# Sliding-window attention inside a four-layer kernel: vector operations over four rows at once, and the query copy moved

## Chip, cores and metric

The kernel runs on one core of one Trainium2 chip. The metric is the device time of one execution in microseconds (us); a kernel's time is the median of its runs.

## What is computed

Four residual layers stand one after the other, attention, Fourier mixing, attention, Fourier mixing, on x of 2048 rows by 640 columns in float32, each behind a layer normalisation. The attention is local and dilated: 32 heads of 20 columns, and each row sees 8 rows, itself and those 2, 4, ... 14 rows before it.

```python
qkv = (x @ wqkv) split in q, k, v, 32 heads of 20
idx = pos[:, None] - arange(8)[None, :] * 2          # masked where idx < 0
logits = einsum("bhsd,bhswd->bhsw", q, kg) * 20 ** -0.5
attn = softmax(logits, axis=-1)
o = einsum("bhsw,bhswd->bhsd", attn, vg)
x = x + o @ wo                                       # layer A
a = x @ dft_hid_re.T;  b = x @ dft_hid_im.T
x = x + (dft_seq_re @ a - dft_seq_im @ b)            # layer B, on the normalised x
```

## The kernel before

The rows are permuted on the host, even rows first, so that a step of 2 becomes a step of 1. They are cut into 4 chunks of 512 rows; partition p of a chunk holds 4 neighbouring rows, j = 0 to 3. All matmuls are done in three passes over a high and a low float32r part of each operand (`PASSES`); ACT makes the high part (`t_hi`, `c_hi`, `ln_hi`) and DVE or POOL the low one by a subtraction (`c_lo` L901, `wo_lo` L555, `ln_lo` L866).

**A layer of attention (`layer_a`).** PE makes q, k and v of a chunk's row j and a quarter of the heads per group (`qkv_mm` L354), ACT moves them out of PSUM (`qkv_evac` L361), and DMAs store them to DRAM. From there they come back as windows: one contiguous piece per partition of 11 rows holds all that 4 query rows need (`w_load` L409), in a ring of 5 slots named `win`. The window arithmetic does not use PE. It is cut into 32 units u, 8 for each chunk; a unit is 4 heads (80 columns, `FE`) for 4 rows per partition. In the last chunk, units 24 to 31 (`PAIRED`), a unit is 8 heads for 2 rows, with two windows of 9 rows a side; the chunk's first row pair is then finished before its second.

Each unit goes through these steps, most of them twice, once for each half of two rows (`jp`):
- `q_load` and `q_copy` (L396, ACT): the query comes from DRAM into tile `qs` and is copied into the PSUM bank `pq`. The same bank holds the mask, the maximum, the sum and the probabilities `pp`, in other columns.
- `qk_mul`: DVE multiplies query and key window into a product of 2 x 8 x 80 = 1280 elements per partition (L423), POOL adds the first 10 columns of each head to the last 10 (L425).
- `qk_red`: DVE sums those 10 into the logits (L431).
- `soft` parts 0 to 2 on DVE (mask, maximum, subtraction), `soft_exp` on ACT (L439), parts 3 to 5 on DVE (sum, reciprocal, probabilities L456). These are done once per unit.
- `av_mul`: DVE multiplies probabilities and value window (L461).
- `av_tree`: POOL sums the 8 window rows pairwise in three steps, L476, L477 and L478, the last into the output tile `oo` (`zo`). The last half of the last unit is summed on DVE.

The products lie in four tiles `pr0` to `pr3` of 1280 elements taken in turn (`prod`), keys' and values' products mixed.

The output is transposed on PE, split, multiplied by wo (`wo_mm` L501), added to x by DVE (`wo_add` L151) and stored. While a layer of attention runs, PE also starts the next Fourier layer's first product (`z_mm` L916), whose matrix is split by `c_hi` and `c_lo` in the first layer of attention and read back split in the second.

**The order.** Everything in a layer of attention is issued in an order written out by hand, on all engines. `at(step, phase, fn, ...)` enters a call into a plan; the steps run from -7 to 66, and within a step the phases run in the order of `PHASES`. Each engine's queue is in that order, so an instruction that waits holds up what stands behind it on its engine. Unit u has steps 2u and 2u + 1 for its two halves of `qk_mul`; the logit sums follow a step later (`red1`, `red0`), the first half of the softmax and the exponent are at 2u + 2, the second half at 2u + 3, and the two halves of `av_mul` and `av_tree` at 2u + 3 (`av1`) and 2u + 4 (`av0`). `q_copy` of unit u is at step 2u - 1 in phase `qc`, behind `av1` and behind ACT's own phases. The last transposes of a layer are at step `TA` = 65 and after the loop (67).

The Fourier layers use the same tiles again: `load_w` puts four of the five parts of the imaginary matrix into `pr0` to `pr3`, and the first chunk's input rows are loaded into `pr0` to `pr3` at the start of the kernel.

Of the kernel before, what the change touches and what calls it, by code (L numbers as in the profile page):

```python
# [20 lines left out]
D = 640  # L21
H = 32
DH = 20
# [25 lines left out]
)  # L49
TA = 65  # L50
NWARM = 18
# [20 lines left out]
def tile_layers(ctx: ExitStack, tc: tile.TileContext, x, wqkv, wo, cs, wre, wim, out):  # L72
# [161 lines left out]
    def layer_a(li, stats, handoff, prev):  # L234
# [6 lines left out]
        xnT = {}  # L241
        pcnt = [0]
        mt = {}
# [14 lines left out]

        def prod():
            pcnt[0] += 1  # L260
            return T([P, 2, W, FE], f"pr{pcnt[0] % 4}")

# [136 lines left out]
        def w_load(u, t, i=None):  # L399
            c = u // NE  # L400
            e, jp = half(u, i or 0)
            r0 = (c % 2) * 512
            if i is not None:
                r0 += 2 * jp
            n = SLOTS if i is None else SLOTS - 2
            b = kvb[e // 2][c // 2][e % 2, t, r0 : r0 + n, :]
            src = bass.AP(tensor=b.tensor, offset=b.offset, ap=[[NJ * FE, P], [1, n * FE]])
            w = wtile([P, SLOTS * FE])
            nc.sync.dma_start(w[:, : n * FE], src)  # L409
            if i is None:  # L410
                for x in range(2):
                    win[(u, x, t)] = (w, 2 * x * FE)
            else:
                win[(u, i, t)] = (w, 0)
# [5 lines left out]
        def qk_mul(u, jp):  # L420
            pr = prod()
            q = qs[u][:, 2 * jp : 2 * jp + 2].unsqueeze(2).to_broadcast([P, 2, W, FE])
            nc.vector.tensor_tensor(pr, q, wview(u, jp, 0, [[1, FE]]), op=ALU.mult)  # L423
            pv = pr.rearrange("p j w (h d) -> p (j w h) d", d=DH)
            nc.gpsimd.tensor_tensor(pv[:, :, 0:10], pv[:, :, 0:10], pv[:, :, 10:20], op=ALU.add)  # L425
            prq[(u, jp)] = pv

        def qk_red(u, jp):
            if jp == 0:
                lgs[u] = T([P, NJ, W, HE], "lg", bufs=2)  # L430
            nc.vector.tensor_reduce(  # L431
                lgs[u][:, 2 * jp : 2 * jp + 2].rearrange("p j w h -> p (j w h)"),
                prq.pop((u, jp))[:, :, 0:10],
                axis=AX.X,
                op=ALU.add,
            )
# [21 lines left out]

        def av_mul(u, jp):
            pr = prod()  # L460
            nc.vector.tensor_tensor(  # L461
                pr.rearrange("p j w (h d) -> p j w h d", d=DH),
                lgs[u][:, 2 * jp : 2 * jp + 2].unsqueeze(4).to_broadcast([P, 2, W, HE, DH]),
                wview(u, jp, 1, [[DH, HE], [1, DH]]),
                op=ALU.mult,
            )
            avq[(u, jp)] = pr

        def av_tree(u, i):
            c = u // NE  # L470
            e, jp = half(u, i)
            if e == 0:
                oo[(c, jp)] = T([P, 2, D], f"zo{(2 * c + jp) % 4}")
            pr = avq.pop((u, i))
            g = nc.vector if (u, i) == (NG - 1, 1) else nc.gpsimd
            g.tensor_tensor(pr[:, :, 0:4], pr[:, :, 0:4], pr[:, :, 4:8], op=ALU.add)  # L476
            g.tensor_tensor(pr[:, :, 0:2], pr[:, :, 0:2], pr[:, :, 2:4], op=ALU.add)  # L477
            g.tensor_tensor(oo[(c, jp)][:, :, e * FE : (e + 1) * FE], pr[:, :, 0], pr[:, :, 1], op=ALU.add)  # L478

# [123 lines left out]
        def prologue_first():  # L603
            wq_begin(0)
            for j, (k0, k1) in enumerate(((0, 3), (3, 5))):
                x_load(0, j, f"pr{j}")
                for k in range(k0, k1):
                    wq[(0, k)] = wq_load1(0, k)
            for j in range(2, NJ):
                x_load(0, j, f"pr{j}")  # L610
            for q in (1, 2, 3):
# [144 lines left out]
        for c, w, xtags in (  # L756
# [3 lines left out]
            for j in range(NJ):  # L760
                if c == 2:
                    tp(48, "o", c, j, 0, 3, ("xt", "t0", "t1", "m0")[j], 0, ("ot", "s1", "r1_2", "r1_2")[j])
                    tp(52, "o", c, j, 3, 5, f"aux{j // 2}", 256 * (j % 2))
                else:
                    tp(58 if j < 2 else TA, "o", c, j, 0, 3, f"aux{j % 2}", 0, ("ot", "s1", "zo0", "zo1")[j])
                    tp(60 if j < 2 else 67, "o", c, j, 3, 5, "aux0" if j < 2 else "pq", 256 * (j % 2))
                if j < len(w):
# [8 lines left out]
        for ph in ("peT0", "hi", "peL", "actL"):  # L776
            plan.pop((67, ph))
        at(66, "pe3w", wo_mm, c, 2, ("aux0", "aux1"), 0, 2, 0, 3)
        for i in range(2):
            at(65, "dmas", *((handoff.cw_load, 0) if first else (handoff.c_get,)), 14 + i)  # L780
        at(65, "dmar", r_load, c, 2, "xr")
        at(66, "dmar", r_load, c, 3, "xa")
# [4 lines left out]
        last = 66  # L787
        thirds = [t for t, n in ZTHIRDS[ly].items() for _ in range(n)]
# [14 lines left out]
        else:  # L803
            at(63, "dmac", handoff.c_get, 13)

        PHASES = (
            "peT0 dma evac hi pe peL pe2 fin red0 dma2 qk sA sB av0 sD red1 sE sC exp evacA actL evacO actl sF av1 qc"
            " dmaw dmas misc dmac dmar pe3w pe3"
        ).split()
        with tc.manual_schedule(engines=ENGINES):  # L810
# [7 lines left out]
            pc_pe(67)  # L818
            pc_hi(67)
            pc_lo(67, True)  # L820
            wo_mm(c, 2, None, 0, 2, 3)
# [22 lines left out]
    class LayerB:  # L844
# [79 lines left out]
        def load_w(self):  # L924
            self.wr = T([P, 2, KD, D], "r2a", F32R)
            self.wi = []
            for k in range(KD):
# [3 lines left out]
                if k < 4:  # L931
                    wt = T([P, 2, D], f"pr{k}", F32R)
                    hl = (wt[:, 0], wt[:, 1])
# [383 lines left out]
```

## Time and profile before

| | us |
|---|---|
| median of 3 runs (lowest to highest) | 1812.42 (1808.80 to 1813.48) |
| the profiled execution's own time | 1810.4 |
| its span, first to last instruction | 1808.5 |
| PE busy, DVE busy, ACT busy, POOL busy | 1746.1, 1380.1, 818.9, 640.6 |
| L423 and L461, DVE, 128 times each | 189.8 and 190.8 busy, mean 1483 and 1491 ns |
| L431, DVE, 128 times | 103.9 busy, mean 811 ns |
| L425, L476, L477, POOL | 183.4, 200.9, 114.4 busy, mean 1433, 1595, 908 ns |

PE is TensorE, DVE VectorE, ACT ScalarE, POOL GpSimd, SP SyncE, which issues most DMAs. A busy time is summed over the whole span, which holds two layers of attention and two Fourier layers; POOL works almost only in the attention. A line of the profile names the source line of the kernel before (L423), what an instruction writes and reads, and, in square brackets or behind an arrow, how long its engine was idle ahead of it and what ended that. Granted clock is the share of full speed that the throttle allows PE.

### The profile page before, as it was taken

The numbers are of one execution on the slowest core, as the hardware profiler recorded it, in microseconds if no ns is written. First come the engines' busy times: TensorE is split into PE (matmuls) and PEld (weight loads), VectorE is DVE, ScalarE is ACT, GpSimd is POOL, SyncE is SP. The second block draws the span as 40 slices with busy tenths as digits, with TensorE's granted clock in tenths as the row PEclk, the third lists the DMA queues.
The fourth block names the chain that finished last, engine by engine and source line by source line (L and its number), as shares of the span: only waits on it lengthen the run. The fifth ranks groups of instructions, "written<-read, shape, count | busy, mean of one in ns | idle before, by whom it ended". The sixth has DMA issues, their size and how long they took to land.

```text
span 1808.5 us, 26471 instructions
## 1 busy us (share of the span) xinstructions
PE 1746.1 (97%) x8798; PEld 1508.9 (83%) x8798; DVE 1380.1 (76%) x2129; ACT 818.9 (45%) x1708; POOL 640.6 (35%) x597
## 2 busy tenths in 40 slices
PE   9999997989999999999999999999899999999999
PEld 6879886777887887888888889877788888888888
DVE  5899899888768767767739988887777677676673
ACT  5544544544445445445533334444434443443441
POOL 3799898960000000000008987899400000000000
PEclk9999998999999999999999999999999999999999
DMA  6776667647789689677647856687687766876761
GB/s 233 224 263 208 208 203 247 218 164 280 273 267 332 223 270 336 221 258 229 215 132 226 278 181 199 200 296 261 218 295 257 259 226 225 265 231 223 259 210 52
DMA packets 273738, 423.59 MB, mean 234 GB/s; under 512 B 22688, under 2 KB 152736, under 8 KB 273344
## 3 DMA queue, kind: packets, MB, share of 16 engines
q1 hardware_dynamic: 270400, 419.92, 70.0%
q10 hardware_dynamic: 3200, 1.97, 0.4%
q8 instruction: 70, 1.15, 0.2%
q14 instruction: 68, 0.56, 0.1%
HBM read 336.66 MB, written 85.14 MB: 233 GB/s over the span
## 4 chain that ended last, share of the span: by engine, by line
PE 65%; DVE 12%; DMA 10%; POOL 6%; ACT 3%; issue 3%; SPq 1%; DVEq 0%; ACTq 0%; POOLq 0%
PE m L354 17%; PE aux L994 13%; PE t L1083 9%; PE m L1083 9%; PE xt L1083 4%; PE pq L1083 4%; PE aux L501 4%; DMA win<-cs_in 2%; DVE pr L423 2%; DVE pr L461 2%; PE m L916 2%; PE t L916 2%; POOL pr L476 2%; DMA c0b<-r 2%; DVE r L1077 1%
## 5 line engine op out<-in xcount | busy, mean ns | idle before, releaser
L354 PE MATMUL m<-r,s 128*128 128x480 f32 x1920 | 439.9, 384 | 5.7 <-ACT s L224 2.4
L354 PEld LDWEIGHTS m<-r,s 128*128 128x128 f32 x1920 | 357.5, 189 | 61.5 <-ACT s L224 3.8
L166 POOL TENSOR_TENSOR stats<-stats,mhalf 128x1 f32<-128x1 f32 (+1 forms) x40 | 30.4, 761 | 564.9 <-ACT stats L162 564.8
L1076 ACT CAST r<-win 128x512 fp32r<-128x512 f32 x244 | 149.4, 620 | 178.4 <-DVE win L1112 75.5
L994 PE MATMUL aux<-r2a,zo 128*128 128x320 f32 x768 | 226.5, 310 | 0.0
L476 POOL TENSOR_TENSOR pr<-pr 128x640 f32<-128x640 f32 x126 | 200.9, 1595 | 40.7 <-DVE pr L461 39.7
L423 DVE TENSOR_TENSOR pr<-pq,win 128x1280 f32<-128x1280 f32 x128 | 189.8, 1483 | 29.9 <-ACT pq L396 29.3
L994 PE MATMUL aux<-pr,zo 128*128 128x320 f32 x704 | 208.2, 308 | 0.0
L1077 DVE TENSOR_TENSOR r<-win,r 128x512 fp32r<-128x512 f32 x244 | 164.5, 686 | 46.8 <-ACT r L1076 40.7
L461 DVE TENSOR_TENSOR pr<-pq,win 128x1280 f32<-128x1280 f32 x128 | 190.8, 1491 | 4.5 <-DVE pq L456 0.2
L425 POOL TENSOR_TENSOR pr<-pr 128x640 f32<-128x640 f32 x128 | 183.4, 1433 | 18.7 <-DVE pr L423 15.6
L1083 PE MATMUL m<-r,r 128*128 128x512 f32 x600 | 154.7, 392 | 0.4 <-DVE r L1077 0.4
L994 PEld LDWEIGHTS aux<-r2a,zo 128*128 128x128 f32 x768 | 144.1, 188 | 2.0
L1083 PE MATMUL t<-r,r 128*128 128x512 f32 x498 | 135.4, 393 | 2.5 <-issue 2.5
L916 PE MATMUL m<-s,r 128*128 128x512 f32 x384 | 119.8, 399 | 15.3 <-DMA s<-c0b 6.7
L1083 PEld LDWEIGHTS m<-r,r 128*128 128x128 f32 x600 | 112.4, 188 | 25.8 <-DVE r L1077 0.7
L994 PEld LDWEIGHTS aux<-pr,zo 128*128 128x128 f32 x704 | 132.1, 188 | 2.0
L916 PE MATMUL t<-s,r 128*128 128x512 f32 x384 | 118.4, 395 | 2.3 <-DVE ot L976 1.5
L361 ACT COPY stg<-m 128x480 f32<-128x480 f32 x128 | 70.9, 556 | 104.6 <-PE m L354 94.0
L477 POOL TENSOR_TENSOR pr<-pr 128x320 f32<-128x320 f32 x126 | 114.4, 908 | 9.9
L431 DVE TENSOR_REDUCE lg<-pr 128x64 f32<-128x640 f32 x128 | 103.9, 811 | 17.7 <-POOL pr L425 17.4
L1083 PEld LDWEIGHTS t<-r,r 128*128 128x128 f32 x498 | 93.4, 188 | 24.6 <-issue 3.3
(269 smaller groups left out, 3246.3 us busy)
## 6 DMA issues: line engine op xcount, KB each, us to landing
win<-cs_in SPq DMA_DIRECT2D x358, 256.0 KB, 4.1
r<-xc SPq DMA_DIRECT2D x240, 256.0 KB, 4.3
win<-kvb SPq DMA_DIRECT2D x96, 440.0 KB, 4.8
xa<-cs_in SPq DMA_DIRECT2D x124, 256.0 KB, 4.2
win<-kvb SPq DMA_DIRECT2D x64, 360.0 KB, 5.3
xc<-stg SPq DMA_DIRECT2D x40, 512.0 KB, 3.1
kvb<-stg SPq DMA_DIRECT2D x60, 320.0 KB, 3.9
xr<-xs SPq DMA_DIRECT2D x40, 320.0 KB, 3.2
```

The costliest lines, as they stand in the source:

```text
L354: nc.tensor.matmul(mt[g][:, : 3 * F], st[:, a, k], wq[q][:, b, k], start=n == 0, stop=n == 14)
L423: nc.vector.tensor_tensor(pr, q, wview(u, jp, 0, [[1, FE]]), op=ALU.mult)
L425: nc.gpsimd.tensor_tensor(pv[:, :, 0:10], pv[:, :, 0:10], pv[:, :, 10:20], op=ALU.add)
L431: nc.vector.tensor_reduce(lgs[u][:, 2 * jp : 2 * jp + 2].rearrange("p j w h -> p (j w h)"), prq.pop((u, jp))[:, :, 0:10], axis=AX.X, op=AL ...
L461: nc.vector.tensor_tensor(pr.rearrange("p j w (h d) -> p j w h d", d=DH), lgs[u][:, 2 * jp : 2 * jp + 2].unsqueeze(4).to_broadcast([P, 2, ...
L476: g.tensor_tensor(pr[:, :, 0:4], pr[:, :, 0:4], pr[:, :, 4:8], op=ALU.add)
L477: g.tensor_tensor(pr[:, :, 0:2], pr[:, :, 0:2], pr[:, :, 2:4], op=ALU.add)
L916: self.last = nc.tensor.matmul(self.z[t][k], self.xn[c][:, a, j, k * P : (k + 1) * P], self.ct[s][:, b], start=s == 0 and i == 0, stop=s = ...
L994: self.last = nc.tensor.matmul(self.ym[e][:, :320], zt[(k, a, ri)][:, j2 * P : (j2 + 1) * P], w[:, e * 320 : (e + 1) * 320], start=(k, a, ...
L1076: nc.scalar.copy(hi, raw)
L1077: nc.vector.tensor_tensor(lo, raw, hi.bitcast(F32), op=ALU.subtract)
L1083: nc.tensor.matmul(bank, w(a, kb), hl[b], start=start and (a, b) == (0, 0), stop=stop and (a, b) == (1, 0),)
```

## The change

In the attention each vector operation is issued once per unit over 2560 elements, where it was issued per half over 1280. `qk_mul` writes one product tile `prA`, `av_mul` one product tile `prB`; each has one buffer of 2560 elements, and together they take the room of `pr0` to `pr3`. In the units of `PAIRED` the two products of a side stay separate instructions, one for each window, but write into one tile, so that POOL's additions and the logit sums are issued once. L478 stays two instructions, since its output goes to different places. The last unit's tree stays in halves, the first on POOL, the second on DVE.

The order changes with it: `qk_mul` at step 2u, the logit sums, the first half of the softmax and the exponent at 2u + 1, the second half at 2u + 2, the probability product and the tree at 2u + 3. Within a step the phases on DVE are now query product, second half of the softmax, probability product, logit sums, first half of the softmax; the query copy stands between the probability product and the logit sums, and the exponent last among ACT's phases. The last steps of a layer come one earlier. In the paired units both windows of a side are loaded at one step.

```diff
-TA = 65
+TA = 64
...
-        def prod():
-            pcnt[0] += 1
-            return T([P, 2, W, FE], f"pr{pcnt[0] % 4}")
+        def prod(tag):
+            return T([P, NJ, W, FE], tag)
...
-        def wview(u, i, t, tail):
-            w, off = win.pop((u, i, t))
-            return bass.AP(tensor=w.tensor, offset=w.offset + off, ap=[w.ap[0], [FE, 2], [FE, W]] + tail)
...
+        def wviews(u, t, tail):
+            paired = u in PAIRED
+            for i in range(1 + paired):
+                w = win.pop((u, i if paired else None, t))
+                js = slice(2 * i, 2 * i + 2) if paired else slice(0, NJ)
+                yield js, bass.AP(tensor=w.tensor, offset=w.offset, ap=[w.ap[0], [FE, js.stop - js.start], [FE, W]] + tail)
+
+        def qk_mul(u):
+            pr = prod("prA")
+            for js, w in wviews(u, 0, [[1, FE]]):
+                q = qs[u][:, js].unsqueeze(2).to_broadcast([P, js.stop - js.start, W, FE])
+                nc.vector.tensor_tensor(pr[:, js], q, w, op=ALU.mult)
             pv = pr.rearrange("p j w (h d) -> p (j w h) d", d=DH)
             nc.gpsimd.tensor_tensor(pv[:, :, 0:10], pv[:, :, 0:10], pv[:, :, 10:20], op=ALU.add)
-            prq[(u, jp)] = pv
+            prq[u] = pv
+
+        def qk_red(u):
+            lgs[u] = T([P, NJ, W, HE], "lg", bufs=2)
             nc.vector.tensor_reduce(
-                lgs[u][:, 2 * jp : 2 * jp + 2].rearrange("p j w h -> p (j w h)"),
-                prq.pop((u, jp))[:, :, 0:10],
...
+                lgs[u].rearrange("p j w h -> p (j w h)"), prq.pop(u)[:, :, 0:10], axis=AX.X, op=ALU.add
             )
...
+        def av_mul(u):
+            pr = prod("prB")
+            for js, w in wviews(u, 1, [[DH, HE], [1, DH]]):
+                nc.vector.tensor_tensor(
+                    pr[:, js].rearrange("p j w (h d) -> p j w h d", d=DH),
+                    lgs[u][:, js].unsqueeze(4).to_broadcast([P, js.stop - js.start, W, HE, DH]),
+                    w,
+                    op=ALU.mult,
+                )
+            avq[u] = pr
...
+            pr = avq.pop(u)
+            for js in (slice(0, 2), slice(2, 4)) if u == NG - 1 else (slice(0, NJ),):
+                g = nc.vector if js.start else nc.gpsimd
+                g.tensor_tensor(pr[:, js, 0:4], pr[:, js, 0:4], pr[:, js, 4:8], op=ALU.add)
+                g.tensor_tensor(pr[:, js, 0:2], pr[:, js, 0:2], pr[:, js, 2:4], op=ALU.add)
+                for i in range(js.start // 2, js.stop // 2):
+                    e, jp = half(u, i)
+                    v = pr[:, 2 * i : 2 * i + 2]
+                    g.tensor_tensor(oo[(c, jp)][:, :, e * FE : (e + 1) * FE], v[:, :, 0], v[:, :, 1], op=ALU.add)
...
-                    at(2 * u + i - 2, "dmaw", w_load, u, 0, i)
-                    at(2 * u + i + 1, "dmaw", w_load, u, 1, i)
+                    at(2 * u - 2, "dmaw", w_load, u, 0, i)
+                    at(2 * u + 1, "dmaw", w_load, u, 1, i)
...
             at(2 * u - 1, "qc", q_copy, u)
             at(2 * u - 2, "dma", q_load, u)
-            for jp in range(2):
-                s = 2 * u + jp
-                at(s, "qk", qk_mul, u, jp)
-                at(s + 1, "red0" if jp else "red1", qk_red, u, jp)
-                at(s + 3, "av0" if jp else "av1", av_mul, u, jp)
-                at(s + 3, "av0" if jp else "av1", av_tree, u, jp)
+            at(2 * u, "qk", qk_mul, u)
+            at(2 * u + 1, "red", qk_red, u)
             for i, ph in enumerate(("sA", "sB", "sC")):
-                at(2 * u + 2, ph, soft, u, i)
-                at(2 * u + 3, ("sD", "sE", "sF")[i], soft, u, 3 + i)
-            at(2 * u + 2, "exp", soft_exp, u)
+                at(2 * u + 1, ph, soft, u, i)
+                at(2 * u + 2, ("sD", "sE", "sF")[i], soft, u, 3 + i)
+            at(2 * u + 1, "exp", soft_exp, u)
+            at(2 * u + 3, "av", av_mul, u)
+            at(2 * u + 3, "av", av_tree, u)
...
         PHASES = (
-            "peT0 dma evac hi pe peL pe2 fin red0 dma2 qk sA sB av0 sD red1 sE sC exp evacA actl evacO actl sF av1 qc"
+            "peT0 dma evac hi pe peL pe2 fin dma2 qk sD sE sF av qc red sA sB sC evacA actl evacO actl exp"
             " dmaw dmas misc dmac dmar pe3w pe3"
         ).split()
```

Beside this, the first chunk's four input tiles become slices of one tile in `prA`, and `load_w` puts two parts of its matrix into each of `prA` and `prB`.

More of the change, by code (lines that the diff above doesn't have):

```diff
@@ L241, in layer_a @@
         xnT = {}
-        pcnt = [0]
         mt = {}
@@ L409, in w_load @@
             nc.sync.dma_start(w[:, : n * FE], src)
[L410 to L414, printed above, removed]
[L416 to L423 removed]
+            win[(u, i, t)] = w
+        def wviews(u, t, tail):
[9 more added lines that the diff above has]
+                nc.vector.tensor_tensor(pr[:, js], q, w, op=ALU.mult)
             pv = pr.rearrange("p j w (h d) -> p (j w h) d", d=DH)
             nc.gpsimd.tensor_tensor(pv[:, :, 0:10], pv[:, :, 0:10], pv[:, :, 10:20], op=ALU.add)
[L426 to L430 removed]
+            prq[u] = pv
+        def qk_red(u):
+            lgs[u] = T([P, NJ, W, HE], "lg", bufs=2)
             nc.vector.tensor_reduce(
[L432 to L435 removed]
+                lgs[u].rearrange("p j w h -> p (j w h)"), prq.pop(u)[:, :, 0:10], axis=AX.X, op=ALU.add
             )
@@ L457, in soft, with av_tree @@
                 lgs[u] = pp
[L459 to L469, printed above, removed]
-            c = u // NE
[L471 to L478, printed above, removed]
+        def av_mul(u):
[8 more added lines that the diff above has]
+            avq[u] = pr
+        def av_tree(u):
+            c = u // NE
+            for i in range(2):
+                e, jp = half(u, i)
+                if e == 0:
+                    oo[(c, jp)] = T([P, 2, D], f"zo{(2 * c + jp) % 4}")
+            pr = avq.pop(u)
[4 more added lines that the diff above has]
+                for i in range(js.start // 2, js.stop // 2):
+                    e, jp = half(u, i)
+                    v = pr[:, 2 * i : 2 * i + 2]
+                    g.tensor_tensor(oo[(c, jp)][:, :, e * FE : (e + 1) * FE], v[:, :, 0], v[:, :, 1], op=ALU.add)
         def r_load(c, j, tag="xr"):
@@ L776, in layer_a @@
         for ph in ("peT0", "hi", "peL", "actL"):
-            plan.pop((67, ph))
-        at(66, "pe3w", wo_mm, c, 2, ("aux0", "aux1"), 0, 2, 0, 3)
+            plan.pop((66, ph))
+        at(65, "pe3w", wo_mm, c, 2, ("aux0", "aux1"), 0, 2, 0, 3)
         for i in range(2):
-            at(65, "dmas", *((handoff.cw_load, 0) if first else (handoff.c_get,)), 14 + i)
-        at(65, "dmar", r_load, c, 2, "xr")
-        at(66, "dmar", r_load, c, 3, "xa")
+            at(64, "dmas", *((handoff.cw_load, 0) if first else (handoff.c_get,)), 14 + i)
+        at(64, "dmar", r_load, c, 2, "xr")
+        at(65, "dmar", r_load, c, 3, "xa")
         if prev is not None:
@@ L786, in layer_a @@
                 at(j2 - 2, "actl", prev.yout, NT - 1, j2, stats)
-        last = 66
+        last = 65
         thirds = [t for t, n in ZTHIRDS[ly].items() for _ in range(n)]
@@ L817, in layer_a @@
                         fn(*args)
-            pc_pe(67)
-            pc_hi(67)
-            pc_lo(67, True)
+            pc_pe(66)
+            pc_hi(66)
+            pc_lo(66, True)
             wo_mm(c, 2, None, 0, 2, 3)
```

16 lines of the change are left out of this document (11 added, 5 removed).

## The prediction

> **What bounds the kernel now.** The page's first part comes first: PE is busy for 97% of the span, so nearly all that an edit of DVE and POOL work can win lies in the time in which PE waits.
>
> ```profile
> PE 1746.1 (97%) x8798; PEld 1508.9 (83%) x8798; DVE 1380.1 (76%) x2129; ACT 818.9 (45%) x1708; POOL 640.6 (35%) x597
> POOL 3799898960000000000008987899400000000000
> ```
>
> The POOL line of the 40 slices shows where the two attention layers lie, about 32 to 395 us and 939 to 1292 us. The table of windows inside them:
>
> ```profile
> core 0: us, PE busy (x) PEld busy (x) DVE busy (x) ACT busy (x) POOL busy (x), PEclk, DMA share, GB/s
> 228.00:310.00 82.00, 71.60 (x372) 62.38 (x372) 76.07 (x110) 36.15 (x94) 74.33 (x68) 0.95 0.71 223
> 1000.00:1170.00 170.00, 170.00 (x880) 151.61 (x880) 148.49 (x211) 67.95 (x168) 146.75 (x136) 0.99 0.67 215
> 1184.00:1266.00 82.00, 73.43 (x397) 63.65 (x397) 67.81 (x107) 35.41 (x90) 78.08 (x72) 0.98 0.82 278
> 67.00:112.00 45.00, 40.12 (x181) 33.47 (x180) 42.14 (x53) 20.21 (x49) 37.39 (x35) 0.96 0.80 258
> ```
>
> From 1000 to 1170 us PE never stops: what DVE or POOL save there is worth nothing (112 to 228 us is alike, PE 115.2 of 116). In 67:112 and 228:310 DVE is full but for the gaps between instructions and PE waits; in 1184:1266 POOL is full (78.1 of 82), and the chain of waits runs through POOL alone:
>
> ```profile
> 1226.56 1.40 POOL pr L425
> 1227.95 1.54 POOL pr L476
> 1229.56 0.90 POOL pr L477
> 1230.53 0.53 POOL zo L478
> 1231.06 1.53 POOL r L866
> 1232.59 0.52 POOL stats L166
> 1233.11 1.40 POOL pr L425
> ```
>
> One half unit takes POOL 6.55 us there, a unit 13.1. The chain shows POOL also from 343 to 372 us. PE's idle time in both layers' attention, summed over 10 us windows, is 41 us: the ceiling, but for time at a lowered clock.
>
> **The change, term by term, against the profiled execution's 1810.4 us** (span 1808.5 and 1.9 around it). The median shown, 1812.42, is 2.0 above it; I add that at the end.
>
> *Term 1, fewer DVE instructions.* The products L423 and L461 take 1483 and 1491 ns for 1280 elements, the softmax's L446 277 ns for 128: 1.047 ns an element and 143 ns fixed. But L423 begins 1.40 us before its independent successor (39.37 to 40.77), 1.34 of that being elements, so between independent neighbours only 60 ns is saved. A merge is worth 60 to 143 ns; I take 100. A unit of the first three chunks merges two products and one reduction; the last eight units keep two products per side, since their windows are two tiles, and merge only L431. DVE-paced are 4.3 units (67:112) and 7.8 (228:310, the last two of them paired): 10.1 x 3 + 2 = 32 merges x 0.1 = -3 us (2 to 4.6). Elsewhere PE or POOL covers it.
>
> *Term 2, fewer POOL instructions.* L476, L477 and L478 take 1.595, 0.908 and 0.533 us for 640, 320 and 160 elements; the short two give 2.3 ns an element and 160 to 190 ns fixed. L425, L476 and L477 merge in every unit but the last, whose tree stays in halves; L478 stays two: 0.56 us of 13.1 a unit. POOL-paced are 82 / 13.1 = 6.3 units in layer two and about 2.3 in layer one: 8.6 x 0.56 = 4.8 us. DVE, busy for 68 of 82 us there, can follow, but each unit now has bigger lumps to hand over: I take -4 (0 to 4.8).
>
> *Term 3, the query copy.* It writes the PSUM bank that the probability product reads, and it waits for that product although the columns differ. Before, the product of an odd step is DVE's last big one, the copy comes behind all of ACT's step, and the next step's L423 needs it. First what L423's engine waited for (us, times), then the timeline, then a window:
>
> ```profile
>   ACT pq L396: 29.3, 17
> ```
>
> ```profile
> 304.59 0.43 ACT L396 COPY pq<-qs 128x320 f32<-128x320 f32 x1 [4.71 <-DVE pr L461]
> 305.64 0.58 PE L327 MATMUL aux<-ot,nident 128*128 128x256 f32 x1 [2.47 <-ACT s L323]
> ```
>
> ```profile
> 305.00:310.00 5.00, 1.59 (x5) 1.25 (x6) 4.93 (x7) 2.80 (x11) 4.76 (x6) 0.50 0.73 231
> ```
>
> L423 waited 29.3 us for it, 17 times. Afterwards the copy (0.43 us) runs while DVE makes the logit sums (two of 0.81 less the fixed part, 1.48 us), and the first that needs it is the mask or maximum behind them; that hides it unless ACT is over 0.9 us late. Most of the 29.3 us lies where PE paces; in 67:112 and 228:300 the waits are 1.9 and 1.8: -3 with some of the rest. The timeline and the window show a second harm: ACT, held 4.71 us by the copy, reached the casts L323 late, PE idled 2.47 and then 2.76 us for ACT (5.2), and its granted clock was 0.62, 0.50 and 0.51 in 300:305, 305:310 and 310:315: 3.17 + 1.59 + 5.00 us of work at about 0.53, 4.6 lost; 9.8 in all. In the new order neither copy nor exponent stands in ACT's even steps, where these casts are. But DVE is also late for PE there, so I take 3 of the 9.8. Term 3 is -6 (0 to 13). SP gains too: the query load L393 waited 58.0 us (15 times) for the copy in layer one; no separate price.
>
> *Term 4, longer POOL instructions in the way of DVE.* A DVE subtraction with both inputs in SBUF waits for the POOL instruction running:
>
> ```profile
> 79.28 1.57 POOL L476 TENSOR_TENSOR pr<-pr 128x640 f32<-128x640 f32 x1 [0.72 <-DVE pr L461]
> 79.31 2.22 DVE L555 TENSOR_TENSOR r2a<-zo,r2a 128x640 fp32r<-128x640 f32 x1
> 80.93 1.34 POOL L477 TENSOR_TENSOR pr<-pr 128x320 f32<-128x320 f32 x1
> 86.10 0.81 DVE L555 TENSOR_TENSOR r2a<-zo,r2a 128x640 fp32r<-128x640 f32 x1
> 86.26 2.07 POOL L476 TENSOR_TENSOR pr<-pr 128x640 f32<-128x640 f32 x1 [1.83 <-DVE pr L461]
> ```
>
> L555 takes 0.81 us when it starts first and 2.22 when L476 does: it ends 0.68 us after L476. The Trainium skill has a rule for this ("SBUF — State Buffer", section "Who interferes with whom"): such a DVE operation and a GpSimd read exclude each other for a whole instruction, and the first to start wins; the trace agrees (2.22 against 0.81). The products are exempt, one input being in PSUM. L901 (14 times, 15.5 us against 14 x 0.68) and L555 (5 times, 7.5 against 5 x 0.81), all in layer one, now lose 9.4 us. Weighted by length, what is left of a POOL instruction met at random is 0.63 us for the four of a half unit and 1.16 for the five merged ones (2.7, 2.97, 1.6, 0.53, 0.53): 19 x 0.53 = +10 at worst if POOL is always busy and DVE always paces. L555 falls mostly in a paced window, L901 about half: +5 (0 to +10).
>
> *Term 5, the end of each layer.* The plan is one step shorter. Between the last query product's end (377.35) and the last tree's (392.67) lie 15.3 us. Afterwards I count from that end: softmax 0.95, product of unit 30 2.98, logit sums 1.48, maximum and subtraction 0.7, small work 0.7, softmax 0.95; meanwhile POOL's whole tree of unit 30 (2.97 + 1.6 + 1.07 = 5.6 from 3.95) ends at 9.6, and only then may the last product write the same tile: 2.98, then DVE's half tree 2.75: 15.3 again. The starting point comes earlier, since 3.2 us of DVE work (a half reduction, a half product, a softmax half) now lies behind it; against that POOL has no half unit to start on. -1 per layer, -2 (-6 to +4).
>
> *At nothing:* the paired units' second window load moves a step earlier, both issues back to back on SP; 360 KB land in 5.3 us, needed two steps (10 us) later, with five window slots in turn. If SP blocked on a slot, the query load and chunk loads behind it would be late, up to 5 us once. The first inputs' four tiles become slices of one: their readers finish before the first product at 34.0.
>
> Sum: -3 - 4 - 6 + 5 - 2 = -10, 1800.4 for the profiled execution, 1802 as a median. The ends add up to -28 and +12.
>
> **Rivals.**
>
> *The single product buffer couples POOL and DVE (slower).* Before, two half buffers serve the probability products and DVE fills one while POOL sums the other. Now the product of unit u+1 waits for the whole tree of u (5.6 us), and queued behind it on DVE are the next logit sums, the softmax, the output additions and the splits that PE waits for; the exponent on ACT waits for the softmax, and the next step's casts behind it. POOL keeps busy only if DVE's product (2.83 to 2.98) ends before POOL is through with the next query add (2.7) and one L866 with L166 (2.05): DVE may reach the product at most 1.8 us after the tree's end. Beyond that POOL stands for the excess. Per unit DVE needs about 9.05 us besides small work and locks, POOL 8.4 and up to 4.1: with three output additions (0.56 each) and one L901 DVE is past that point. If half a product, 1.4 us, is lost in each of the 13 units from 290 to 372 and 1184 to 1266, that is +18, and term 2's 4 go: 1824. For: POOL already waited 39.7 us for L461. Against: most such waits were 0.7 us, and a DVE-paced unit has no need of a second buffer.
>
> *The gains fall where PE paces, waits behind POOL take the rest (no change).* With each of the 19 subtractions meeting a merged POOL instruction as the one at 79.31 met a half one, term 4 is +10, and term 3 keeps its 3 us alone: -3 - 4 - 3 + 10 - 2 = -2, 1810. The Trainium skill's rule of whole-instruction exclusion ("SBUF — State Buffer", "Who interferes with whom") leads to this rival rather than to the forecast. For: PE is 97% busy. Against: layer two has no L901 or L555 in these windows.
>
> That the change doesn't do what it says: the paired units do keep two products, which term 1 has in it.
>
> **How the numbers follow.** About 0.3%, 5.4 us, is what a measurement of this kernel tells from no change. Forecast 0.5 (1802, its own range 1788 to 1807), coupling 0.33, no change 0.17. The range reaches from 1788, short of the sum's far end, to the coupling's 1824: 1788 to 1824.
>
> **What would show it.** L423 and L461 at 2560 elements near 2.82 us, 24 of these and 16 of half size per layer; L476 near 2.97 us; L423 no more waiting for L396; PE's idle time from 290 to 315 us at least 3 us less, with the clock nearer 1; L901 and L555 up by about 5 us in sum; POOL's period from 1226 us at 12.5 a unit. The forecast is wrong if L461 waits long for L478, if POOL's idle before L476 grows past 40 us, or if the splits reach PE later than now.

## The result and the profile after

| | before | after |
|---|---|---|
| median of 18 runs each, us | 1811.73 | 1819.52 |
| lowest to highest, us | 1808.80 to 1814.97 | 1812.55 to 1826.72 |
| ratio, 95% interval | 1 | 1.0042 [1.0031, 1.0052] |
| profiled execution (span), us | 1810.4 (1808.5) | 1814.24 (1812.5) |

The changed kernel is slower by 7.8 us, where 10 us less had been forecast. Its profiled execution lies 5 us under its own median, so that profile shows half of the loss at most, and the sizes below come from the ratios of runs. A second profile of the changed kernel (g1, 1820.14 us) has the same waits: 87.3 us where 85.5 stands below, and the same 29.8 for the subtractions.

The page's engines, after:

```profile
PE 1749.9 (97%) x8798; PEld 1511.2 (83%) x8798; DVE 1385.3 (76%) x1969; ACT 820.2 (45%) x1708; POOL 603.8 (33%) x409
```

DVE has 160 instructions fewer and POOL 188, and POOL is busy for 36.8 us less. DVE is not: 5.2 us more. PE does the same matmuls. Two groups of instructions (busy us, mean ns; then idle time ahead of them and what ended it) show what a merged instruction takes; the second counts one half instruction of each layer's last unit too:

```profile
L421 DVE TENSOR_TENSOR prA<-pq,win 128x2560 f32<-128x2560 f32 x48 | 135.3, 2818 | 2.4 <-ACT pq L394 1.8 <-DMA win<-kvb 0.6
L473 POOL TENSOR_TENSOR prB<-prB 128x1280 f32<-128x1280 f32 x64 | 186.4, 2913 | 85.8 <-DVE prB L456 85.6
```

(L421, L456, L473, L394 after are L423, L461, L476, L396 before; L359, L352 and L321 are L361, L354 and L323.) POOL now stands 85.6 us ahead of the first addition of the tree for DVE's product, 39.7 before. The windows, with the columns as before:

```profile
67.00:112.00 45.00, 38.54 (x167) 32.03 (x166) 42.79 (x42) 20.45 (x49) 34.96 (x24) 0.92 0.77 256
228.00:310.00 82.00, 76.67 (x391) 66.65 (x389) 74.34 (x86) 34.93 (x89) 66.15 (x42) 0.96 0.70 220
1000.00:1170.00 170.00, 166.97 (x860) 148.68 (x861) 146.22 (x162) 68.76 (x169) 137.71 (x88) 0.99 0.67 215
```

Two of them lose. In 67:112 PE is busy for 38.54 us in place of 40.12, at a clock of 0.92 in place of 0.96. In 1000:1170 PE stood still for nothing before; now it is idle for 3 us, all of it before 1030 us, and the two waits named there are for ACT's normalised rows (L183) and its high part of a transpose (L321). In 228:310 PE does 5 us more.

Where the query copy stands now is told by the trace of its line (L396 before, L394 after): how long ACT was idle ahead of it, and until what (us, times), before and after:

```profile
  DVE pr L461: 42.4, 23
```

```profile
  DVE prB L456: 85.5, 30
```

And who waited for it, after:

```profile
  DVE lg L440: 12.3, 8
  DVE pq L442: 8.5, 6
```

With 1.8 us at L421, DVE still waits 22.6 us for the copy, 29.3 before, only at other instructions. ACT's wait at the copy has doubled. But ACT also waits for DVE at the exponent, and there it waits far less than before (us in total, times, longest; the third line is of f4 below, the changed kernel without the copies):

```profile
ACT lg L439 <- DVE lg L450: 145.9, 52, 7.0
ACT lg L433 <- DVE lg L444: 36.8, 30, 3.1
ACT lg L434 <- DVE lg L445: 93.0, 37, 7.5
```

At both places together ACT waited 188.3 us before and waits 122.3 us after.

The subtractions with both inputs in SBUF, in layer one's attention (L905 after is L901 before), two groups before and three after:

```profile
L901 DVE TENSOR_TENSOR s<-stg,s 128x512 fp32r<-128x512 f32 x14 | 15.5, 1118 | 0.0
L555 DVE TENSOR_TENSOR r2a<-zo,r2a 128x640 fp32r<-128x640 f32 x4 | 6.1, 1513 | 0.0
```

```profile
L905 DVE TENSOR_TENSOR s<-stg,s 128x512 fp32r<-128x512 f32 x14 | 19.1, 1374 | 0.0
L555 DVE TENSOR_TENSOR r2a<-zo,r2a 128x640 fp32r<-128x640 f32 x4 | 7.5, 1882 | 0.0
L555 DVE TENSOR_TENSOR r2a<-ot,r2a 128x640 fp32r<-128x640 f32 x1 | 3.2, 3225 | 0.0
```

With 1.4 us for the fifth of L555, they took 23.0 us before, and now take 29.8. A stretch of the timeline of after (start, duration, and in brackets the idle time of the engine ahead of it):

```profile
93.97 0.43 ACT L394 COPY pq<-qs 128x320 f32<-128x320 f32 x1 [4.73 <-DVE prB L456]
96.50 0.31 ACT L433 ACTIVATE lg<-lg 128x128 f32<-128x128 f32 x1 [1.44 <-DVE lg L444]
96.72 1.00 ACT L359 COPY stg<-m 128x480 f32<-128x480 f32 x2
97.31 8.34 PE L352 MATMUL m<-r,s 128*128 128x480 f32 x30 [2.83 <-ACT stg L359]
...
100.42 2.66 POOL L423 TENSOR_TENSOR prA<-prA 128x1280 f32<-128x1280 f32 x1 [0.30 <-DVE prA L421]
101.37 2.39 DVE L555 TENSOR_TENSOR r2a<-zo,r2a 128x640 fp32r<-128x640 f32 x1
106.57 0.43 ACT L394 COPY pq<-qs 128x320 f32<-128x320 f32 x1 [8.86 <-DVE prB L456]
107.54 4.65 PE L352 MATMUL m<-r,s 128*128 128x480 f32 x13 [1.90 <-ACT stg L359]
```

ACT stands at the copy for 4.73 us, then at the exponent for 1.44; the evacuation L359 that PE needs comes behind both, and PE idles 2.83. Then POOL starts L423 first, the subtraction L555 takes 2.39 us and ends 0.68 us after it, DVE's next product is that much later (1.58 us over the 0.81 that the subtraction takes alone), ACT stands at the next copy for 8.86 us, and PE idles again. The clock falls with it: in 95:100 PE is busy for 2.69 us, at 0.75. Such a spell stood here before the change too (90:95, busy for 3.21 us, at 0.80).

That the wait at the copy is what makes PE idle here is not borne out by f4. Without the copies ACT stands at the exponent in the same place for 6.31 us, the evacuation comes behind it just as late (97.12 us), and PE's waits for L359 up to 112 us are 4.0 us, 4.7 with the copies; PE is busy for 38.36 us in 67:112. By 112 us PE has begun 470 matmuls before the change and 454 after; without the copies (f4) it is 462, without the subtractions (f2) 480. So what is lost up to there goes with the subtractions, and half of it with the copies.

### The profile page after: what moved, and what is told of

It reads as the page before. It is cut to its first block, busy times and chain, and to the rows that moved or that the text cites. A ratio compares the mean times of both kernels' runs of the same rounds, so it can differ in the third digit from the quotient of the medians.

```text
span 1812.5 us, 26097 instructions
## 1 busy us (share of the span) xinstructions
PE 1749.9 (97%) x8798; PEld 1511.2 (83%) x8798; DVE 1385.3 (76%) x1969; ACT 820.2 (45%) x1708; POOL 603.8 (33%) x409
## 4 chain that ended last, share of the span: by engine, by line
PE 65%; DVE 14%; DMA 9%; POOL 7%; ACT 3%; issue 2%; SPq 0%; DVEq 0%; ACTq 0%; POOLq 0%
PE m L352 16%; PE aux L1000 13%; PE t L1089 9%; PE m L1089 9%; PE xt L1089 4%; PE pq L1089 4%; DMA win<-cs_in 3%; PE aux L501 3%; DVE prB L456 3%; DVE prA L421 2%; POOL prB L473 2%; PE t L920 2%; PE m L920 1%; POOL prA L423 1%; DVE r L1083 1%
## 5 line engine op out<-in xcount | busy, mean ns | idle before, releaser
L352 PE MATMUL m<-r,s 128*128 128x480 f32 x1920 | 441.1, 385 | 7.7 <-ACT stg L359 4.7
L352 PEld LDWEIGHTS m<-r,s 128*128 128x128 f32 x1920 | 359.2, 190 | 63.1 <-ACT stg L359 5.7
L473 POOL TENSOR_TENSOR prB<-prB 128x1280 f32<-128x1280 f32 x64 | 186.4, 2913 | 85.8 <-DVE prB L456 85.6
L456 DVE TENSOR_TENSOR prB<-pq,win 128x2560 f32<-128x2560 f32 (+1 forms) x80 | 181.6, 2286 | 6.8 <-POOL zo L478 3.8
L421 DVE TENSOR_TENSOR prA<-pq,win 128x2560 f32<-128x2560 f32 (+1 forms) x80 | 181.4, 2283 | 2.4 <-ACT pq L394 1.8
L423 POOL TENSOR_TENSOR prA<-prA 128x1280 f32<-128x1280 f32 x64 | 170.7, 2668 | 16.4 <-DVE prA L421 16.2
L359 ACT COPY stg<-m 128x480 f32<-128x480 f32 x128 | 71.0, 556 | 154.1 <-PE m L352 126.9
L1000 PE MATMUL aux<-prA,zo 128*128 128x320 f32 x384 | 114.0, 307 | 0.0
L1082 ACT CAST s<-win 128x512 fp32r<-128x512 f32 x116 | 71.3, 620 | 80.7 <-DVE win L1118 24.2
L474 POOL TENSOR_TENSOR prB<-prB 128x640 f32<-128x640 f32 x64 | 102.0, 1594 | 5.0
L1118 DVE TENSOR_TENSOR win<-win,win 128x512 f32<-128x512 f32 x111 | 76.5, 691 | 35.5 <-DMA win<-cs_in 34.1
```

The source lines that it names most:

```text
L352: nc.tensor.matmul(mt[g][:, : 3 * F], st[:, a, k], wq[q][:, b, k], start=n == 0, stop=n == 14)
L421: nc.vector.tensor_tensor(pr[:, js], q, w, op=ALU.mult)
L456: nc.vector.tensor_tensor(pr[:, js].rearrange("p j w (h d) -> p j w h d", d=DH), lgs[u][:, js].unsqueeze(4).to_broadcast([P, js.stop - js. ...
L473: g.tensor_tensor(pr[:, js, 0:4], pr[:, js, 0:4], pr[:, js, 4:8], op=ALU.add)
L474: g.tensor_tensor(pr[:, js, 0:2], pr[:, js, 0:2], pr[:, js, 2:4], op=ALU.add)
L1000: self.last = nc.tensor.matmul(self.ym[e][:, :320], zt[(k, a, ri)][:, j2 * P : (j2 + 1) * P], w[:, e * 320 : (e + 1) * 320], start=(k, a, ...
```

## The experiments

Three theories. A: the query copy. ACT, in order, waits at it for a product that is now twice as long, and what PE and DVE need stands behind it. B: POOL's longer additions hold DVE's subtractions in SBUF up for longer. C: bigger lumps and the single product buffer cost by themselves, whatever waits. All ratios are to the kernel before, run beside each on the same chip (its medians there 1814.5 to 1816.0 us), from 5 to 12 runs of each. In `PHASES`, `actL` (the low parts of the transposes) and `actl` are two phases; the diff ahead of the prediction writes both as `actl`.

### Places of the copy, and POOL in halves

```diff
 e1, after: PHASES
-sF av qc red sA sB sC evacA actL evacO actl exp
+sF av evacA actL evacO qc red sA sB sC actl exp
 e2, before: PHASES
-qk sA sB av0 sD red1 sE sC exp evacA actL evacO actl sF av1 qc
+qk sA sB av0 sD red1 sE sC sF av1 qc exp evacA actL evacO actl
```

> The changed kernel with one edit: on ACT the evacuations of the matmul banks and the low parts of the transposes (phases evacA, actL, evacO) come ahead of the query copy; the copy itself stays between the probability product and the logit sums, and DVE's, POOL's and PE's order is untouched. Theory A (the copy, waiting for the doubled product, holds ACT, and the evacuations behind it starve PE): PE's wait for the evacuation (4.7 us in layer one) goes, and the time falls by 4 to 8 us, to 1.000 to 0.998 of the kernel before. Theory B (DVE waits for longer POOL instructions) and theory C (one product buffer and large lumps): no change from the changed kernel, 1.003 to 1.005 of before.

> The kernel before with one edit: its last softmax part, its odd step's probability product and the query copy stand ahead of ACT's phases of the step, so that on ACT the copy is ahead of the evacuations as in the changed kernel; all other queues keep their order and all operations their half size. Theory A: slower than before by 4 to 10 us (1.002 to 1.006), with PE waiting for the evacuation. Theories B and C: no change or a gain of up to 4 us from the earlier copy (0.998 to 1.000).

e1, with the copy behind the evacuations: 1823.87 us, 1.0051 [1.0031, 1.0071], nothing won back, where theory A expected 0.998 to 1.000. ACT's wait for the product fell from 85.5 to 66.4 us, and DVE's for the copy rose from 22.6 to 28.8; PE's waits for L359 in layer one, which were to go, are still 4.3 us of 4.7. e2 puts the copy of the kernel before ahead of ACT's own work, as after: 1821.29 us, 1.0037 [1.0022, 1.0052], as theory A expected (1.002 to 1.006). ACT's wait at the copy rose from 42.4 to 86.6 us (at the exponent, now behind the copy, it fell from 145.9 to 76.9), while DVE's for the copy fell from 29.3 to 7.5: so this move alone makes the old kernel slower by nearly as much as the whole change does, although the wait that the prediction counted on is mostly gone.

```diff
 e3, after: POOL's additions twice over half of the merged tile
-            nc.gpsimd.tensor_tensor(pv[:, :, 0:10], pv[:, :, 0:10], pv[:, :, 10:20], op=ALU.add)
+            for i in range(2):
+                hv = pv[:, 64 * i : 64 * i + 64]
+                nc.gpsimd.tensor_tensor(hv[:, :, 0:10], hv[:, :, 0:10], hv[:, :, 10:20], op=ALU.add)
...
-            for js in (slice(0, 2), slice(2, 4)) if u == NG - 1 else (slice(0, NJ),):
-                g = nc.vector if js.start else nc.gpsimd
+            for js in (slice(0, 2), slice(2, 4)):
+                g = nc.vector if js.start and u == NG - 1 else nc.gpsimd
 e4: e3, and DVE's products and logit sums in halves too, in the new order
```

> The changed kernel with POOL's additions (query add and tree) issued for two rows at a time again, as before, while DVE's products and sums stay merged. POOL's longest instruction is 1.58 us again instead of 2.9. Theory B: the subtractions with both inputs in SBUF (wo_lo and c_lo) lose about 5 us less in sum, and the time falls by 4 to 8 us. Theory A: up to 3 us slower than the changed kernel, since POOL pays its fixed part again. Theory C: within 2 us of the changed kernel.

> The changed kernel's order, tiles and steps, but every product, sum and addition is issued for two rows at a time, so that no operation is merged. If the loss lies in the order (theory A, and theory C as far as it is the single buffer), it is as slow as the changed kernel or slower, 1.003 to 1.008 of before. If it lies in the doubled size (theory B), it is back within 3 us of the kernel before.

e3: 1816.96 us, 1.0008 [0.9995, 1.0021]: 0.34% won back by issuing more instructions on POOL. The subtractions in e3's groups:

```profile
L907 DVE TENSOR_TENSOR s<-stg,s 128x512 fp32r<-128x512 f32 x14 | 18.1, 1302 | 0.0
L557 DVE TENSOR_TENSOR r2a<-zo,r2a 128x640 fp32r<-128x640 f32 x4 | 4.6, 1158 | 0.0
```

With the fifth (0.8 us) that is 23.5 us, as before the change. e4: 1818.22 us, 1.0018 [1.0004, 1.0031]: DVE's merging is worth some 0.10%, 1.8 us by the middle values, which the intervals do not separate from nothing.

### Without the subtractions, without the copy

```diff
 f1 (before) and f2 (after), in short: L901 (L905) and L555
-            nc.vector.tensor_tensor(<low part>, <operand>, <high part>, op=ALU.subtract)
+            nc.vector.memset(<low part>, 0.0)
 f3 (before) and f4 (after)
-            nc.scalar.copy(qp, qs[u])
+            if u == 0:
+                nc.scalar.copy(qp, qs[u])
```

> The kernel before, in which the low parts of wo and of the first Fourier matrix's blocks (L555 and c_lo) are left out: a memset on DVE stands in their place, so that no DVE instruction of the attention in layer one has two inputs in SBUF. Base for the next run. 19 subtractions with 23.0 us of DVE time in the profile go, memsets of an estimated 0.4 to 0.8 us each come: 5 to 12 us faster than before where DVE paces (0.993 to 0.998).

> The changed kernel with the same leaving-out. Theory B (DVE waits for POOL instructions of double length, 29.8 us of DVE time against 23.0): the loss against the run before it shrinks from 8 us to 0 to 3 us, ratio to f1 1.000 to 1.0015. If the order of the copy (theory A) or the single product buffer (theory C) is the cause: the loss stays, ratio to f1 1.003 to 1.005.

f1: 1811.91 us, 0.9982 [0.9971, 0.9993], a gain of 3 us, less than the 5 to 12 expected (the memsets take 0.49 and 0.59 us each); f2: 1814.92 us, 0.9996 [0.9984, 1.0008]. The loss from the old kernel to the new shrinks from 0.42% to 0.14%: some 5 us of it hang on these subtractions, B.

> The kernel before without the query copy: only the first unit's query is copied, all others are multiplied with it, so ACT's 63 other copies and every wait for them and by them are left out. Measures what the copy costs before. The prediction's term 3 (a gain of 6 us from hiding it): 4 to 10 us faster than before, 0.995 to 0.998. Theory A: little, 0.998 to 1.000, since the copy last in ACT's step holds little.

> The changed kernel without the query copy, as above. Prediction's term 3 (the copy is hidden now): no change from the changed kernel, 1.003 to 1.005 of before, and DVE gains nothing. Theory A (the copy ahead of the evacuations holds ACT): 5 to 9 us faster than the changed kernel, 0.999 to 1.001 of before, PE's waits for the evacuation L359 gone.

f3: 1813.52 us, 0.9987 [0.9976, 0.9999]; f4: 1812.25 us, 0.9979 [0.9968, 0.9989]. The copy costs 0.13%, 2.4 us, in the old order and 0.63%, 11 us, in the new. Without it the changed kernel is no slower than the old one. f4's gain is more than theory A expected (0.999 to 1.001), but not by the way that it named: PE's waits for L359 stayed. In 1000:1170, PE is busy for 168.28 us in f4, against 166.97 with the copy. Another way in which the copy could cost is through SP, whose query loads wait for it before they write `qs` again; but SP waited 88.5 us (30 times) there before, and waits 31.9 us (17 times) after.

### The copy on DVE

```diff
-            nc.scalar.copy(qp, qs[u])
+            nc.vector.tensor_copy(qp, qs[u])
```

> The changed kernel as it is, on the chip and beside the runs of before that the next three share. All theories: 1.003 to 1.006 of before.

> The changed kernel with the query copy made by DVE at the same place in the order, between the probability product and the logit sums, so that ACT neither makes it nor waits for a product, and DVE has 64 more instructions, an estimated 0.2 to 0.5 us each. Theory A (the copy holds ACT): 3 to 9 us faster than the changed kernel, the 11 us that leaving the copy out gave less what DVE pays in the stretches it paces: 0.998 to 1.002 of before. If the gain of leaving it out came from DVE's work or the query loads: no change or slower, 1.004 or more.

> Both suspected causes taken away while the computation stays whole: the changed kernel with POOL's additions in halves and the query copy made by DVE. Theories A and B together: faster than the kernel before by 2 to 8 us, 0.996 to 0.999. Only one of them: within 2 us of the run that takes that one away alone, about 1.000 to 1.001.

> The kernel before with the query copy made by DVE, at its old place behind the odd step's probability product. Theory A (before, the copy cost only the 2 us that leaving it out gave): DVE's additional 64 instructions cancel that, 0.999 to 1.003 of before.

The changed kernel beside them (g1): 1823.03 us, 1.0042 [1.0030, 1.0055]. With DVE's copy (g2): 1820.49 us, 1.0021 [1.0008, 1.0035], although DVE spends 64 x 0.495 = 31.7 us on it. The same edit makes the old kernel slower (g4): 1819.75 us, 1.0030 [1.0014, 1.0045]. So in the new order the copy on ACT costs the kernel more than 31.7 us of DVE's work do, in the old one less. g3, with POOL in halves too: 1814.85 us, 0.9997 [0.9984, 1.0011], the best of the changed kernels that leave nothing out, and no better than the kernel before; the 0.996 to 0.999 expected of both cures was not reached.

### One cause or two

```diff
 h1: f2 with POOL's additions in halves, as in e3
 h2: e3 without the copies, as in f4
 h3: e3, in halves in layer one only
+            n = 2 if first else 1
+            for i in range(n):
 h4: h3 with the copy on DVE
```

> The changed kernel with the low parts of wo and of the Fourier blocks left out (memsets in their place, as in f2) and POOL's additions in halves. Theory B: with no instruction left that waits for POOL's port, halves bring nothing: 0.9996 to 1.0010 of before, as f2 (0.9996) or up to 2 us slower for POOL's additional fixed parts. Theory C (large lumps and one product buffer, which halves ease): 3 us or more faster than f2, 0.998 or less.

> The changed kernel with POOL's additions in halves and the query copy left out (all units use the first unit's query). Both suspected causes are gone. If A and B are separate costs: 0.9950 to 0.9970 of before, at least 2 us below f4 (0.9979). If they are one chain (DVE late by the lock makes the copy late, which holds ACT): no better than f4, 0.9970 to 0.9985.

> The changed kernel with POOL's additions in halves in the first layer of attention only, where all 19 subtractions with two SBUF inputs lie; merged in the second, where POOL paces for some 80 us. Theory B: as fast as halves everywhere (e3, 1.0008) or up to 4 us faster by POOL's saved fixed parts: 0.9985 to 1.0008. If the loss by merged additions lies in both layers: between e3 and the changed kernel, 1.0015 to 1.003.

> As h3, with the query copy made by DVE. Theories A and B with term 2's saving in layer two: 0.997 to 0.9995 of before. If DVE's 31.7 us of copies eat what ACT gains: 1.000 to 1.002.

h1: 1817.75 us, 1.0014 [1.0001, 1.0027], against f2's 0.9996. With no subtraction left to hold up, halves on POOL win nothing; by the middle values they cost 0.18%, 3 us. So what e3 won back goes through the subtractions, B, and C falls as far as POOL's lumps go; the single product buffer stands in every kernel of the new order, and no run takes it away alone. h2: 1807.62 us, 0.9957 [0.9942, 0.9971], the furthest under the old kernel, and 0.51% under e3: A and B nearly add up (0.63% and 0.34% alone, 0.85% together). h3: 1816.33 us, 1.0011 [0.9997, 1.0025], as e3: B lies in layer one, where L905 and L555 are. h4: 1816.38 us, 1.0005 [0.9991, 1.0019], not to be told from h3 or g3, and short of the 0.997 to 0.9995 expected.

The profiles place B as well. PE begins the output product of layer one's last row (L501 into `pq`) at 395.7 us before, at 398.9 and 400.2 in two profiles of the changed kernel, at 393.8 in e3 and 393.4 in h3; without the subtractions it is 386.7 in the old order (f1) and 385.0 in the new (f2). So the delay at the end of layer one goes when POOL's additions are halved there or the subtractions are left out; it goes without the copies too (392.8 in f3, 392.9 in f4). At the end of layer two the two profiles of the changed kernel themselves differ by 6.6 us (1293.6 and 1300.2), and single profiles tell no more.

### The copy behind the softmax

```diff
 i1, after; i2, h3: PHASES
-sF av qc red sA sB sC evacA actL evacO actl exp
+sF av red sA sB sC evacA actL evacO actl qc exp
```

> The changed kernel with ScalarE's query copy placed behind the step's evacuations and its part of the softmax, just ahead of the exponent, so that ScalarE stands at VectorE's product at one place of the step only and its earlier work of the step is issued before that. Theory A (the copy costs because ScalarE, in order, waits for the product while evacuations and softmax work wait behind it): 3 to 8 us less than the changed kernel, 0.998 to 1.0025 of the kernel before; ScalarE's wait for the product at the copy well under the 85.5 us that the changed kernel shows. Rival (the copy costs the same wherever it stands, since VectorE's next product needs it): no different from the changed kernel, 1.004 of the kernel before, with VectorE's waits for the copy taking what ScalarE's lose.

> As the run before, with GpSimd's additions in halves in layer one. If both causes are as told (GpSimd's longer additions in layer one, the place of the query copy), their cures add: 0.996 to 0.9995 of the kernel before. If the copy costs the same wherever it stands: 1.001, as with the halves in layer one alone.

i1: 1826.91 us, 1.0058 [1.0044, 1.0071]; i2: 1823.95 us, 1.0034 [1.0021, 1.0046]. Both are slower than with the copy where the change put it. The trace of the copy's line in i1, as above (what ACT waited for, then who waited for the copy):

```profile
  DVE lg L444: 100.0, 36
  DVE prA L421: 43.2, 41
```

Behind the softmax the copy waits for DVE's subtraction L444, which reads the same PSUM bank, and then DVE's next product waits for the copy, 41 times. A's cure by place falls, and so does the rival's forecast that the place changes nothing: the waits moved to DVE and grew.

## Why the prediction was wrong

The runs put the way from the old kernel to the new in four steps, each a difference of ratios, which is known to about 0.2%:

| step | ratio | us |
|---|---|---|
| before, copies left out (f3) | 1 to 0.9987 | -2.4 |
| new order, DVE merged, POOL in halves, still no copies (h2) | to 0.9957 | -5.4 |
| copies back (e3) | to 1.0008 | +9.3 |
| POOL merged (after) | to 1.0042 | +6.2 |

They add up to +7.7. So without the copies the order and DVE's merging do bring something, by the middle values; the copy and POOL's merging take more. The prediction's terms:

- **Term 1**, DVE's fewer instructions, -3. The merged product takes 2.82 us, as forecast. From start to start it is 2.74 us (L456 begins at 103.68, its successor at 106.42), and two halves of 1.40 were 2.80: a merge of products saves 60 ns, not the 100 taken. The logit sums (1.477 us, two of 0.81 before, which stood apart) do better. Measured: -1.8, not separated from 0. The lower end of the price, 60 ns, fits (32 x 0.06 = 1.9 us).
- **Term 2**, POOL's fewer instructions, -4. POOL's period for a unit from 1222 us on is 12.1 us (L423 begins at 1222.38, 1234.97, 1247.36, 1258.70), 13.1 before, and h1 against f2 shows some 3 us by the middle values. But h3, which merges on POOL in layer two alone, where 6.3 of the term's 8.6 units lie, is no faster than e3 (1.0011 and 1.0008). POOL's work is less, as counted; that the time follows is not separated from nothing.
- **Term 3**, the copy hidden, -6: the step that failed, and its sign. It counted DVE's wait for the copy as time won (29.3 us, 17 times) and put what the copy costs in its new place at nothing. It also named its own condition, "unless ACT is over 0.9 us late", and did not price it: DVE still waits 22.6 us for the copy, 15 times, so there ACT is late. And e2 shows that most of that wait can go (to 7.5 us) while the kernel gets slower. In place of a gain the copy's cost rose, by 0.38% (e3 against h2, less that of f3), 7 us, or 0.50%, 9 us, by f4. The second harm it hoped to remove, in 290:315, shrank a little: PE is busy for 17.85 us there, 16.09 before, at a clock of 0.81, 0.73 before.
- **Term 4**, POOL's longer instructions in DVE's way, +5. Mechanism and size in the trace were right: +6.8 us in the 19 subtractions, 0.36 us each, between the 0 and 0.53 of the bounds. As time it is 5 us by f1 and f2; e3 against after shows 6.2 net of term 2's gain, which with the 3 us of that term would make it 9; the intervals don't tell these apart. The Trainium skill's rule ("SBUF — State Buffer", section "Who interferes with whom") says that such a DVE operation and a GpSimd read exclude each other for a whole instruction. The subtraction at 101.37 agrees (2.39 us where it takes 0.81 alone).
- **Term 5**, the end of each layer, -2. The stretch from the last query product's end to the last tree's end was to stay at 15.3 us. It is 18.3 in layer one (377.54 to 395.86) and 18.2 in layer two (1267.32 to 1285.51; 15.0 before): the count had 0.7 us of small work where output additions and subtractions (L151, L905, L870) take more. In layer one it begins no earlier than before, in layer two 4.8 us earlier, yet the last row's output product begins 3.2 and 0.8 us later. Nothing was won.
- **At nothing**, the window loads and the first input tiles: no wait in the profile speaks against it.

The rival that was closest in sign and in number, the coupling by the single product buffer, forecast 1824 but for another reason, so that its nearness is luck: DVE waits only 3.8 us for L478 (L456). One sign listed for it, POOL's wait growing past 40 us, did come (85.6 us), but no run shows that this wait costs anything. The rival without change had half of the truth, term 4 at its upper part, and kept the copy as a gain.

What stays open is why the copy costs four to five times as much in the new order, by the middle values. That it does is shown (f3, f4, h2, e3); that its place within the step is no cure is shown at three places (after, e1, i1). How the cost reaches PE is not shown. ACT's waits for DVE do not tell it: at the copy and the exponent together they fell from 188.3 to 122.3 us. Nor do ACT's and DVE's waits around the copy alone: e2 has 94 us of them and e3 105, both with POOL in halves, and e2 is slower by 0.29%. A query in a PSUM bank of its own, which would free the copy from the product, was not tried.

## What to carry to other kernels

When an operation moves to where nobody waits for its result, price what it holds up in its new place, too: in e2 the receiver's wait fell by 22 us and the time rose. The waits themselves did not foretell this; leaving the operation out in both orders told it. A stall that stands behind a wait in a timeline is that wait's doing only if it goes with it: here PE's waits for L359 outlived the copy. Merging instructions makes them longer for everyone that they lock out; look at how long an instruction of the other engine can stand behind the longest one before counting the fixed cost that is saved. Between independent neighbours on DVE that fixed cost is mostly hidden already (60 of 143 ns were left to save), so compare starts, not durations.

## What was not expected of the hardware

More instructions on POOL made the kernel faster by 0.34% when DVE's subtractions in SBUF stood beside them, and slower by 0.18% by the middle values when they did not. One subtraction of 0.81 us took 3.2 us behind a merged addition (L555 at 112.80, behind L423 at 112.70).

Short stalls of PE can cost more than their length, and the same stall does so in one execution and not in another. Near 916 us, between the attention layers, PE waits for ACT (L224) in all kernels here. In g1 the waits are 1.84 and 0.57 us, the granted clock stays at 1.00, and the 13 matmuls behind them take 3.10 us. In e1 they are 1.82 and 0.57 us, the clock is 0.71 in 916:921 and 0.61 in the next 5 us, and the 13 matmuls take 5.28. The wider scatter of the changed kernel (14.2 us against 6.2 over 18 runs each) is not explained by this: in f3, the old kernel without the copies, the clock falls there too (0.66 in 915:920).

The Trainium skill ("TensorE: Matmul & The Clock Gate", Part 1, on the clock gate) has the clock set from activity in a free-running window of about 3.4 us; that these two stalls came out differently agrees with it, and no run here shows the window itself.
